# Loads of the tiles four ahead, tile 0's keys and values by ScalarE's queue, and the first expert's start inside the last retention tiles

## The chip, the cores and the metric

One core of a Trainium2 chip. The metric is the device time of one execution in microseconds (us); lower is better.

## The reference

Retention over 8 batches, 8 heads, 576 positions and a head width of 64, then a mixture of 16 experts (4 groups of 4), of which each token takes one. All in float32.

```python
scores = scale * np.matmul(q, k.transpose(0, 1, 3, 2))
ret = scores * Dmat[None, :, :, :]            # Dmat[h,i,j] = gamma_h ** (i-j) for i >= j, else 0
x = np.matmul(ret, v)                         # as 4608 tokens x 512
g_idx = argmax(x @ w_group); e_idx = argmax(x[g] @ w_expert[g])
h = np.maximum(x_e @ w1[g, e], 0.0)           # 512 -> 1024
out[tok_idx] = (g_w * e_w)[:, None] * (h @ w2[g, e])   # 1024 -> 512
```

## The kernel before

**Retention.** The tokens are 36 tiles of 128. Each tile has two inputs of 0.5 MB: `a` (queries and keys, transposed) and `b` (keys and values). In the loop's turn t TensorE (PE) makes `pst` (the running state, `state(t)`), `px` (the output of tile t-1, in two parts: `av(t-1)`, `inter(t-1)`), and `pss` (scores of tile t+1); ScalarE (ACT) scales the values (`vs`, eight small instructions) and copies the state (`st`); VectorE (DVE) masks the scores (`sT`) and takes `px` out of PSUM times a table `gq` (`xT`, `turned(t-1)`, line 704). `xT` is feature-major; PE transposes it back (`pxt`, `xnat_pe`, line 335), ACT weights it (`xt`), and GpSimd (POOL) scatters the 128 rows by an indirect DMA into a buffer in HBM, `xs`, one stretch of rows for each expert.

**Routing**, for three tiles at a time: `plt` (`logits`), `lt` (its copy on ACT), `pl` (`gate_pe`), a run of small DVE instructions that ends in `ob` (`choose`, line 385), `pp` (`places_pe`), the slots `sl` (`places`) and the weights `wt` (`weigh`). After tile 26's group (`PICK = 26`) `pick(0)` (line 478) counts the tokens with one small product `pc0` and chooses the expert that goes first; its number `e0i` is what SP reads before it can load that expert's weights. `pad0` is an indirect store that marks the first expert's spare rows.

**Experts.** Sixteen passes p, each with eight slices f: `ph` is layer 1 (`layer1(p, f)`, line 848), `hh` its ReLU, `py` layer 2 (`layer2`, line 888). Weights come as raw pieces `r1_p_i`, `r2_p_i` (512 KB each, two slices to a piece) and are split into a high and a low part (`wh` on ACT, `wl` on DVE), so that most products are made of three. The first pass is different: it takes the first 256 tokens of its expert, and its slices 0 to 5 use the raw weights unsplit. Tokens come back from `xs` as `xb` (`xload`, line 206), are transposed on DVE (`xturn`, line 252, to `xTf`) and split (`xsplit`: `xTh_m` on ACT, `xTl_m` on DVE). An `xb` load waits until the stores into its rows have landed. Results of a pass are transposed by DVE (`y`) and scattered to `out` by POOL. The last pass E = 16 (`last1`, `last_tr`, lines 954 and 970: `phn`, `hn`, `pth`, `hhn`, `py`) takes the rows that pass 0 left.

**What sets the order.** The order on each engine is the order of the calls: a wrapper (`Ordered`, line 106) ties every instruction to the one before it on its engine, so all have line 117 in the profile, and rows are told apart by tile names. SP issues the loads in the order of the calls. `a`, `b`, the weight pieces and `xb` share rings of buffers (tags `r1`, `r2`; `RB = 7`), and each load of a queue also waits for the completion of the load eight before it. Tile loads are asked for `LOADS - 1` = 6 tiles ahead: before the loop tiles 0 to 5, and then one in each turn.

**The places of the change.** Turns 31 to 36 of the loop carry `r = t - 26` = 5 to 10: the pick in t = 31, then `xload(0)` and one weight piece in each of t = 32 to 35, and `xturn(0)` in t = 35. After the loop pass 0 follows, with the routing and the stores of the last tiles between its slices. SP's `xload(1)` stands in slice 3 of pass 0.

Of the kernel before, what the change touches and what calls it, by code (L numbers as in the profile page):

```python
# [66 lines left out]
def moe_retention(ctx, tc, qk, kv, wgt, w1, w2, c_f, out):  # L67
# [779 lines left out]

    def layer1(p, f):
        i = p * NPIECE + f // 2
        C = CS[p]  # L850
        if (p, f) == (0, 0):
            ph = ps_st.tile([P, CMAX], F32, name=f"ph_{p}_{f}", tag="tr")
        elif p == 0:
            ph = psy.tile([P, CMAX], F32, name=f"ph_{p}_{f}", tag=f"py{f % 2}")
        else:
            pool_ = (ps_sm, ps_tr, ps_sm, ps_st)[f % 4]
            ph = pool_.tile([P, CMAX], F32, name=f"ph_{p}_{f}", tag="sm" if f % 2 == 0 else "tr")
        cs = slice((f % 2) * P, (f % 2) * P + P)
        hh = mp.tile([P, CMAX], F32R, name=f"hh_{p}_{f}", tag="hh", bufs=4)
        if whole(p, f):  # L860
            for kc in range(NKC):
                pe.matmul(
                    ph[:, :C], raws[i][0][:, kc, cs], xTf[p][:, kc, :C], start=kc == 0, stop=kc == NKC - 1
                )
            act.activation(hh[:, :C].bitcast(F32), ph[:, :C], AF.Relu)
            hts[p, f] = (hh.bitcast(F32), None)
            return
        wh, wl = wsp[i, 0]
# [498 lines left out]
```

## Time and profile before

| | |
|---|---|
| median of 3 runs | 609.99 us (607.59 to 610.55) |
| the profiled execution | 606.85 us |
| its span in the profile | 605.1 us |
| mean granted TensorE clock | 0.995 |
| PE busy | 584.0 us (97%) |
| DVE, ACT, POOL busy | 430.2 (71%), 325.2 (54%), 263.3 us (44%) |

Busy times are shares of the span of one execution. Starts are counted from the span's start, so the profiled execution's own time is 1.75 us more than its span.

### The profile page before, as it was taken

The page shows a single profiled execution, that of the slowest core. Times are in us where ns is not written, and L with a number is a line of the kernel's source. Part 1 is how long each engine was busy: PE and PEld are TensorE (multiplying, and loading weights), DVE is VectorE, ACT ScalarE, POOL GpSimd, SP SyncE. Part 2 cuts the span into 40 slices and gives each one's busy share as a digit, 9 for nine tenths or more (in the row PEclk, how much of TensorE's full clock was granted, in tenths as well). Part 3 has the DMA queues.
Part 4 walks back from the last instruction along what each step waited for, and adds up shares of the span by engine and source line. Part 5 has one row for each costly group of instructions (what it writes and reads, how often), then busy time and mean ns, then how long its engine had stood idle before and what let it go on. Part 6 is the DMA issues. An engine that isn't in the chain of part 4 may idle for free.

```text
span 605.1 us, 16614 instructions
## 1 busy us (share of the span) xinstructions
PE 584.0 (97%) x6191; PEld 549.7 (91%) x6191; DVE 430.2 (71%) x977; ACT 325.2 (54%) x849; POOL 263.3 (44%) x392
## 2 busy tenths in 40 slices
PE   7889999998999999999999999999999999999995
PEld 7778788777668999999999999999999999999994
DVE  3777677677477666997757675867768677686773
ACT  4677877865346434445435454544545455455553
POOL 0022322333313037494645537373563734636554
PEclk8999999999999999999999999999999999999999
DMA  8999999956983942819465563838467394674921
GB/s 332 416 384 341 344 344 337 353 183 194 381 261 97 349 199 77 298 40 340 111 265 146 230 235 145 284 115 311 130 245 249 123 334 118 259 240 153 369 93 35
DMA packets 62546, 143.11 MB, mean 237 GB/s; under 512 B 9313, under 2 KB 30185, under 8 KB 62464
## 3 DMA queue, kind: packets, MB, share of 16 engines
q1 hardware_dynamic: 53072, 121.59, 57.1%
q0 software_dynamic: 9248, 20.35, 9.4%
q8 instruction: 49, 0.80, 0.5%
q14 instruction: 33, 0.27, 0.1%
q10 hardware_dynamic: 144, 0.10, 0.1%
HBM read 121.67 MB, written 24.88 MB: 242 GB/s over the span
## 4 chain that ended last, share of the span: by engine, by line
PE 87%; DMA 5%; DVE 2%; issue 2%; POOL 1%; ACT 1%; SPq 0%; POOLq 0%; ACTq 0%; DVEq 0%
PE py L117 34%; PE ph L117 34%; PE px L117 7%; PE pss L117 4%; PE pxt L117 3%; PE pst L117 2%; DMA b<-in_kv 2%; PE plt L117 2%; POOL out L117 1%; DMA r<-in_w 1%; DMA xb<-xs 1%; DMA a<-in_qk 1%; PE pl L117 1%; DMA xs<-xt,sl 1%; PE phn L117 0%
## 5 line engine op out<-in xcount | busy, mean ns | idle before, releaser
L117 POOL DMA_INDIRECT out<-y,ii x152 | 167.2, 1100 | 51.0 <-issue 33.8
L117 DVE TENSOR_TENSOR wl<-r,wh 128x512 fp32r<-128x512 f32 x260 | 167.8, 687 | 8.3 <-ACT wh L117 4.5
L117 ACT ACTIVATE hh<-ph 128x356 fp32r<-128x356 f32 (+16 forms) x128 | 53.8, 420 | 212.6 <-PE ph L117 143.1
L117 PE MATMUL ph<-xTh_m,wh 128*128 128x356 f32 (+15 forms) x488 | 147.5, 302 | 0.8 <-ACT xTh_m L117 0.8
L117 ACT CAST wh<-r 128x512 fp32r<-128x512 f32 x260 | 146.9, 617 | 0.0
L117 PE MATMUL ph<-xTl_m,wh 128*128 128x356 f32 (+15 forms) x488 | 146.7, 301 | 0.1
L117 PE MATMUL ph<-xTh_m,wl 128*128 128x356 f32 (+15 forms) x488 | 146.6, 300 | 0.0
L117 PE MATMUL py<-hh,wh 128*128 128x288 f32 (+17 forms) x480 | 145.1, 302 | 0.0
L117 PE MATMUL py<-hl,wh 128*128 128x356 f32 (+14 forms) x480 | 144.7, 301 | 0.0
L117 PE MATMUL py<-hh,wl 128*128 128x356 f32 (+14 forms) x480 | 144.6, 301 | 0.0
L117 DVE SCALAR_TENSOR_TENSOR hl<-ph,hh 128x356 fp32r<-128x356 f32 (+15 forms) x122 | 56.7, 465 | 103.0 <-ACT hh L117 69.9
L117 POOL COPY pace<-hh 1x1 f32<-1x1 f32 x140 | 34.6, 247 | 140.4 <-ACT hh L117 138.4
L117 PEld LDWEIGHTS ph<-xTh_m,wh 128*128 128x128 f32 x488 | 92.0, 189 | 1.7 <-ACT xTh_m L117 1.2
L117 PEld LDWEIGHTS ph<-xTl_m,wh 128*128 128x128 f32 x488 | 92.0, 189 | 0.9 <-DVE xTl_m L117 0.4
L117 PEld LDWEIGHTS ph<-xTh_m,wl 128*128 128x128 f32 x488 | 92.2, 189 | 0.0
L117 PEld LDWEIGHTS py<-hh,wh 128*128 128x128 f32 x480 | 90.5, 189 | 0.2
L117 PEld LDWEIGHTS py<-hl,wh 128*128 128x128 f32 x480 | 90.4, 188 | 0.2 <-DVE hl L117 0.2
L117 PEld LDWEIGHTS py<-hh,wl 128*128 128x128 f32 x480 | 90.5, 189 | 0.0
L117 POOL DMA_INDIRECT xs<-xt,sl x36 | 35.9, 998 | 119.5 <-DVE ob L117 47.1
L117 ACT ACTIVATE vs<-b,cf 128x64 f32<-128x64 f32 x288 | 72.4, 335 | 7.9 <-DMA b<-in_kv 7.9
L117 DVE TENSOR_TENSOR sT<-pss,masks 128x512 f32<-128x512 f32 x72 | 46.0, 681 | 15.9 <-PE pss L117 10.7
L117 PE MATMUL px<-sT,vs 128*64 128x128 f32 x576 | 40.1, 280 | 2.2 <-DVE xT L117 1.7
(167 smaller groups left out, 615.8 us busy)
## 6 DMA issues: line engine op xcount, KB each, us to landing
r<-in_w SPq DMA_DIRECT2D x138, 512.0 KB
a<-in_qk SPq DMA_DIRECT2D x35, 512.0 KB
b<-in_kv SPq DMA_DIRECT2D x35, 512.0 KB
xb<-xs SPq DMA_DIRECT2D x24, 148.5 KB
xb<-xs SPq DMA_DIRECT2D x20, 165.0 KB
out<-y,ii POOLq DMA_INDIRECT x152
xb<-xs SPq DMA_DIRECT2D x12, 181.5 KB
xb<-xs SPq DMA_DIRECT2D x4, 198.0 KB
```

The costliest lines, as they stand in the source:

```text
L117: i_ = f(*a, **k)
```

## The change

- **Loads.** `LOADS` goes from 7 to 5. Tile 0's `b` is issued by ACT, values first, and not by SP; the table `gq` is loaded after tile 1's inputs and not before them; the gate's weights (`wgp`) and the rest of the constants (`cf`) are loaded after tile 3's inputs and not after tile 1's.
- **Turns 31 to 35.** Tile 26's `pxt`, `xt` and store move from t = 32 into t = 31, ahead of `pc0`, with a PSUM buffer of the pool of the small products (`ps_sm`, two buffers). Weight pieces 0 to 3 of the first expert are loaded one turn earlier, the first ahead of `xload(0)`. `xturn(0)` moves from t = 35 to t = 34, and the first product, `layer1(0, 0)`, from behind the loop to t = 35 between `inter(34)` and `turned(34)`.
- **Pass 0.** Its steps are reordered: `ph_0_1` comes first after the loop, `pl_35`, `choose` and `pxt_31` come behind the first `py`, and layer 2 of slice 5 comes ahead of layer 1 of slice 6. Two of the steps that rank the experts, `xpad(2)` and `xload(2)` move from pass 0 into pass 1.
- **Last pass.** `wh1_16_1` and `wl1_16_1` are split one step earlier.

```diff
-LOADS = 7
+LOADS = 5
@@ xnat_pe(t, pool_=None)
+        T["pxt"] = (pool_ or ps_tr).tile(
+            [P, NKC, P], F32, name=f"pxt_{t}", tag="sm" if pool_ else "tr"
+        )
@@ loads, t == 0
+                        if nm == "a":
+                            sp.dma_start(T[nm][:, i], src[nm][t, :, i])
+                        else:
+                            act.dma_start(T[nm][:, 1 - i], src[nm][t, :, 1 - i])
@@ before the loop
-            if t == 0:
+            if t == 1:
                 sp.dma_start(gqs[0], c_f[:, KC_GQ:KC_ALL].rearrange("p (x j) -> p x j", x=4))
-            if t == 1:
+            if t == 3:
                 sp.dma_start(wgp, wgt.rearrange("p (c e) -> p c e", c=NKC))
                 sp.dma_start(cf[:, KC_UP:KC], c_f[:, KC_UP:KC])
@@ the loop
                 inter(t - 1)
+                if r == 9:
+                    layer1(0, 0)
                 turned(t - 1)
...
+            if r == 5:
+                xnat_pe(PICK, ps_sm)
+                xnat_out(PICK)
...
-            if r in (6, 7, 8, 9):
+            if r in (5, 6, 7, 8):
                 if r == 6:
                     xload(0)
-                load_piece(r - 6)
-            if r == 9:
+                load_piece(r - 5)
+            if r == 8:
                 xturn(0, 0, 2)
                 xturn(0, 1, 2)
@@ passes
+            ahead = (p, f) == (0, WHOLE)
+            if ahead:
+                layer2(*prev)
             layer1(p, f)
...
+            if (p, f) == (0, 1):
+                gate_pe(NT - 1)
+                choose(NT - 1)
+                xnat(NT - 5)
             if (p, f) == (0, 2):
+                xnat(NT - 3)
                 tiles_counted()
-                xnat(NT - 2)
-                count_experts()
-            if (p, f) in ((0, 4), (0, 5)):
+            if (p, f) in ((0, 4), (1, 0), (1, 1)):
                 next(ranks, None)
...
+            if (p, f) == (1, 2):
+                xpad(2)
+            if (p, f) == (1, 3):
+                xload(2)
@@ last pass
         if pc == 0:
+            split(2 * E * NPIECE + 3)
             layer2(*prev)
```

On PE, turns 34 to 36 and the start of pass 0, before (`px_35` is in three rows by operand, `pp` left out):

```order
L117 MATMUL pxt_29_3107<-cf_64,xT_27_2494 128x128 x4
L117 MATMUL pl_32_3114<-cf_64,lt_32_3075 128x128 x3
L117 MATMUL px_35_3145<-sT_35_3060,vs_35_3006 64x128 x8
...
L117 MATMUL ph_0_0_3193<-xTf_0_3128,r1_0_0_2899 128x256 x4
...
L117 MATMUL plt_35_3212<-xT_33_3042,wgp_98 32x384 x4
L117 MATMUL pxt_30_3219<-cf_64,xT_30_2747 128x128 x4
L117 MATMUL pxt_31_3230<-cf_64,xT_30_2747 128x128 x4
L117 MATMUL pl_35_3241<-cf_64,lt_35_3217 128x128 x3
...
L117 MATMUL ph_0_1_3258<-xTf_0_3128,r1_0_0_2899 128x256 x4
```

and in the changed kernel:

```order
L117 MATMUL ph_0_0_3115<-xTf_0_3095,r1_0_0_2824 128x256 x4
L117 MATMUL pxt_29_3123<-cf_64,xT_27_2486 128x128 x4
L117 MATMUL pl_32_3130<-cf_64,lt_32_3079 128x128 x3
L117 MATMUL px_35_3152<-sT_35_3064,vs_35_3010 64x128 x8
...
L117 MATMUL ph_0_1_3200<-xTf_0_3095,r1_0_0_2824 128x256 x4
...
L117 MATMUL plt_35_3219<-xT_33_3046,wgp_98 32x384 x4
L117 MATMUL pxt_30_3226<-cf_64,xT_30_2747 128x128 x4
...
L117 MATMUL py_0_0_3260<-r2_0_0_2825,hh_0_0_3116 128x512
L117 MATMUL py_0_1_3261<-r2_0_0_2825,hh_0_0_3116 128x512
L117 MATMUL pl_35_3264<-cf_64,lt_35_3224 128x128 x3
L117 MATMUL pxt_31_3282<-cf_64,xT_30_2747 128x128 x4
```

The first product stands ahead of `px_35`, the second right behind it; `pl_35` is now behind the second product and the first `py`.

On PE in turn 31 (of the change: `pc0` is the small product of the pick, `px_31` is `av(31)`):

```order
L117 MATMUL plt_29_2775<-xT_27_2486,wgp_98 32x384 x4
L117 MATMUL pxt_26_2782<-cf_64,xT_24_2235 128x128 x4
L117 LDWEIGHTS ones_66
L117 MATMUL pc0_2802<-ob_9_2706,ones_66 128x16
L117 MATMUL px_31_2853<-sT_31_2684,vs_31_2620 64x128 x8
```

Before, `pc0` followed `plt_29` directly. `plt`, `pxt_26` and `pc0` now share the two buffers of `ps_sm`, so `pc0` takes the one that `plt_29` held.

On POOL, the last stores into `xs` ahead of pass 1 (of the change; before, `pad1` stood behind the store of `xt_34`):

```order
L117 DMA xs_63<-xt_33_3347,sl_35_3327 75776x528
L117 IOTA xt_34_3372 128x4x4
L117 DMA xs_63<-zero_82,pad1_79 75776x528
L117 IOTA xt_35_3395 64x4x4 x2
L117 DMA xs_63<-xt_34_3372,sl_35_3327 75776x528
L117 DMA xs_63<-xt_35_3395,sl_35_3327 75776x528
```

The store of `xt_35` is the last of the four in both.

## Rows read from the trace of the kernel before

**Rows 1.** The page's busy times: engine, busy us (share of the span), instructions.

```profile
PE 584.0 (97%) x6191; PEld 549.7 (91%) x6191; DVE 430.2 (71%) x977; ACT 325.2 (54%) x849; POOL 263.3 (44%) x392
```

**Rows 2.** Busy time by stretch: the stretch, its length, busy us of each engine (instructions), granted clock, DMA share, GB/s.

```profile
0.00:25.00 25.00, 20.78 (x430) 18.08 (x432) 13.49 (x27) 15.05 (x56) 1.02 (x8) 0.93 0.94 367
130.00:140.00 10.00, 9.15 (x190) 7.19 (x182) 8.33 (x30) 6.56 (x25) 4.65 (x8) 1.00 0.21 81
140.00:150.00 10.00, 8.63 (x179) 6.64 (x180) 7.32 (x22) 5.52 (x18) 3.55 (x6) 1.00 0.77 217
180.00:190.00 10.00, 8.91 (x47) 7.35 (x46) 9.27 (x26) 7.86 (x17) 2.10 (x2) 1.00 0.10 39
595.00:600.00 5.00, 3.31 (x14) 2.15 (x14) 1.07 (x4) 1.31 (x3) 3.06 (x4) 1.00 0.12 36
```

**Rows 3.** The start, ACT: start, us, what, and in brackets the idle time before it and its releaser. The `vs` are those of tiles 2, 4 and 6.

```profile
13.59 2.02 ACT L117 ACTIVATE vs<-b,cf 128x64 f32<-128x64 f32 x8 [1.05 <-DMA b<-in_kv]
...
19.16 2.02 ACT L117 ACTIVATE vs<-b,cf 128x64 f32<-128x64 f32 x8 [0.18 <-DMA b<-in_kv]
21.09 0.35 ACT L117 COPY st<-pst 128x256 f32<-128x256 f32 x1
...
25.20 1.07 ACT L117 ACTIVATE vs<-b,cf 128x64 f32<-128x64 f32 x4
```

**Rows 4.** The start, SP's issues (the first) and PE's states of tiles 2 and 4.

```profile
1.66 0.90 SPq L117 DMA_DIRECT2D b<-in_kv  x2
...
15.91 0.69 PE L117 MATMUL pst<-vs,b 128*64 128x64 f32 x16 [0.79 <-ACT st L117]
...
22.06 0.65 PE L117 MATMUL pst<-vs,b 128*64 128x64 f32 x16
```

**Rows 5.** Busy time by stretch as in group 2, in PE's first long wait and after it.

```profile
6.00:7.00 1.00, 0.00 (x0) 0.00 (x0) 0.98 (x2) 0.00 (x0) 0.00 (x0) 1.00 1.05 367
...
8.00:12.00 4.00, 4.00 (x58) 3.67 (x59) 0.70 (x2) 2.94 (x14) 0.00 (x0) 0.57 1.02 402
```

**Rows 6.** Turn 31: `pc0` and `px_31` on PE, the copy `lt_29` on ACT, the pick's first step, `xT_31` and `sT_33` on DVE.

```profile
131.58 0.18 PE L117 MATMUL pc<-ob,ones 128*128 128x16 bf16 x1
131.69 1.09 PE L117 MATMUL px<-sT,vs 128*64 128x128 f32 x16
...
132.34 0.47 ACT L117 COPY lt<-plt 128x384 f32<-128x384 f32 x1
...
134.65 0.68 DVE L117 TENSOR_TENSOR xT<-px,gq 128x512 f32<-128x512 f32 x1
136.23 1.29 DVE L117 TENSOR_TENSOR sT<-pss,masks 128x512 f32<-128x512 f32 x2 [0.90 <-PE pl L117]
```

**Rows 7.** Turns 34 to 36 and pass 0, PE's waits, and on DVE `xT_34`, `xturn(0)` and `xT_35`.

```profile
147.61 1.09 PE L117 MATMUL px<-sT,vs 128*64 128x128 f32 x16 [0.70 <-DVE xT L117]
150.00 1.97 PE L117 MATMUL ph<-xTf,r 128*128 128x256 f32 x8 [0.67 <-DMA r<-in_w]
154.29 0.66 PE L117 MATMUL pxt<-cf,xT 128*128 128x128 f32 x4 [0.83 <-ACT xt L117]
...
146.87 0.69 DVE L117 TENSOR_TENSOR xT<-px,gq 128x512 f32<-128x512 f32 x1 [2.37 <-PE pxt L117]
147.47 1.29 DVE L117 STREAM_TRANSPOSE xTf<-xb 128x512 f32<-128x512 f32 x2
```

**Rows 8.** Two pieces of SP's issues: the first expert's tokens and weights, and pass 2's tokens; and DVE's transposes of the latter.

```profile
141.39 1.92 SPq L117 DMA_DIRECT2D xb<-xs  x4
...
191.12 2.01 SPq L117 DMA_DIRECT2D xb<-xs  x4
...
206.13 1.76 DVE L117 STREAM_TRANSPOSE xTf<-xb 128x384 f32<-128x384 f32 x3
```

**Rows 9.** The chain that ended last, in order of time, from 165 to 182 us without PE's pieces: start, us, what.

```profile
168.89 3.90 DMA xs<-xt,sl
174.47 4.71 DMA xb<-xs
179.30 1.91 DVE xTf L117 x3
```

**Rows 10.** POOL's stores into `xs` at the end of pass 0 (`xt_33` and `xt_35`), SP's loads of pass 1's tokens, and PE's first product of pass 1.

```profile
164.35 0.99 POOL L117 DMA_INDIRECT xs<-xt,sl  x1 [3.27 <-ACT xt L117]
...
168.89 1.13 POOL L117 DMA_INDIRECT xs<-xt,sl  x1 [0.28 <-issue]
...
172.90 1.89 SPq L117 DMA_DIRECT2D xb<-xs  x4
...
181.77 0.43 PE L117 MATMUL ph<-xTh_m,wh 128*128 128x356 f32 x1 [0.76 <-ACT xTh_m L117]
```

**Rows 11.** The end: DVE's four transposes of pass 15, PE's wait for `wl1_16_1`, the first and the last of POOL's nine stores of pass 15, and its store of the last pass.

```profile
583.91 1.57 DVE L117 STREAM_TRANSPOSE y<-py 128x288 f32<-128x288 f32 x4
588.86 0.39 PE L117 MATMUL phn<-wl,xTh_m 128*128 128x256 f32 x1 [0.39 <-DVE wl L117]
...
585.76 0.97 POOL L117 DMA_INDIRECT out<-y,ii  x1 [6.34 <-DVE y L117]
...
597.31 0.97 POOL L117 DMA_INDIRECT out<-y,ii  x1 [0.30 <-issue]
599.61 0.97 POOL L117 DMA_INDIRECT out<-y,ii  x1 [1.33 <-ACTq L1182]
```

More of the change, by code (lines that the diff above doesn't have):

```diff
@@ L521, in without, with layer1 @@
         dve.tensor_scalar(mi0, sln, picked["c0"], float(BIG), ALU.is_ge, ALU.mult)
+    def layer1(p, f):
+        i = p * NPIECE + f // 2
+        C = CS[p]
+        if (p, f) == (0, 0):
+            ph = ps_st.tile([P, CMAX], F32, name=f"ph_{p}_{f}", tag="tr")
+        elif p == 0:
+            ph = psy.tile([P, CMAX], F32, name=f"ph_{p}_{f}", tag=f"py{f % 2}")
+        else:
+            pool_ = (ps_sm, ps_tr, ps_sm, ps_st)[f % 4]
+            ph = pool_.tile([P, CMAX], F32, name=f"ph_{p}_{f}", tag="sm" if f % 2 == 0 else "tr")
+        cs = slice((f % 2) * P, (f % 2) * P + P)
+        if (p, f) == (0, 0):
+            hh = wp.tile([P, NKC, EARLY], F32, name="hh_0_0", tag="wl0", bufs=3)[:, 0]
+        else:
+            hh = mp.tile([P, CMAX], F32R, name=f"hh_{p}_{f}", tag="hh", bufs=4)
+        if whole(p, f):
+            for kc in range(NKC):
+                pe.matmul(
+                    ph[:, :C], raws[i][0][:, kc, cs], xTf[p][:, kc, :C], start=kc == 0, stop=kc == NKC - 1
+                )
+            hf = hh if f == 0 else hh.bitcast(F32)
+            act.activation(hf[:, :C], ph[:, :C], AF.Relu)
+            hts[p, f] = (hf, None)
+            return
+        wh, wl = wsp[i, 0]
+        xh, xl = xTs[p]
+        n = 0
+        for kc in range(NKC):
+            for a, b in ((wh, xh), (wh, xl), (wl, xh)):
+                pe.matmul(
+                    ph[:, :C], a[:, kc, cs], b[:, kc, :C], start=n == 0, stop=n == 3 * NKC - 1
+                )
+                n += 1
+        C32 = 32 * nblocks(p)
+        if f == 0 and C32 > C and not natural(p):
+            dve.memset(hh[:, C:C32].bitcast(F32), 0.0)
+        hl = mp.tile([P, CMAX], F32R, name=f"hl_{p}_{f}", tag="hl", bufs=4)
+        act.activation(hh[:, :C], ph[:, :C], AF.Relu)
+        dve.scalar_tensor_tensor(
+            hl[:, :C], ph[:, :C], 0.0, hh[:, :C].bitcast(F32), ALU.max, ALU.subtract
+        )
+        hts[p, f] = (hh, hl)
     obs = []
@@ L757, in moe_retention @@
             late_consts(t)
-            if now and 6 <= t:
+            if now and 6 <= t and r != 6:
                 xnat_pe(t - 6)
@@ L771, in moe_retention @@
                 u -= 1
-            for u in range(max(u + 1, 0), t - 5):
+            for u in range(max(u + 1, 0), t - 5 + (r == 5)):
                 if now:
@@ L845, in rank_experts @@
         dve.tensor_scalar(mil, el, cr[:, 0:1], float(BIG), ALU.is_ge, ALU.mult)
[L848 to L868, printed above, removed]
-        xh, xl = xTs[p]
-        n = 0
-        for kc in range(NKC):
-            for a, b in ((wh, xh), (wh, xl), (wl, xh)):
-                pe.matmul(
-                    ph[:, :C], a[:, kc, cs], b[:, kc, :C], start=n == 0, stop=n == 3 * NKC - 1
-                )
-                n += 1
-        C32 = 32 * nblocks(p)
-        if f == 0 and C32 > C and not natural(p):
-            dve.memset(hh[:, C:C32].bitcast(F32), 0.0)
-        hl = mp.tile([P, CMAX], F32R, name=f"hl_{p}_{f}", tag="hl", bufs=4)
-        act.activation(hh[:, :C], ph[:, :C], AF.Relu)
-        dve.scalar_tensor_tensor(
-            hl[:, :C], ph[:, :C], 0.0, hh[:, :C].bitcast(F32), ALU.max, ALU.subtract
-        )
-        hts[p, f] = (hh, hl)
     def layer2(p, f):
```

47 lines of the change are left out of this document (23 added, 24 removed).

## The prediction

> **What bounds the kernel now.** I read the busy times first: PE is busy for 584.0 of the span's 605.1 us [rows 1], so all its idle time together is 21.1 us, and no reordering that leaves PE's work as it is can win more. The change adds no product and takes none away. Then the busy time by stretch, to see where that idle time lies [rows 2]: 25.00 - 20.78 = 4.2 us in the first 25 us, 0.85 + 1.37 = 2.2 us between 130 and 150 us, with a wait of 0.83 behind it [rows 7] 3.05 us, then 1.09 us from 180 to 190, and 1.69 us from 595 to 600. The change touches all four places. Then, for each place, which wait ends last there.
>
> At the start it is a transfer: ACT scales the values of tiles 2 and 4 as soon as they land, at 13.59 and 19.16, and not before tile 6 does it find them there without waiting [rows 3]; PE's state of tile 2 waits for ACT's copy behind the scaling [rows 4]. The DMA engines are busy for 0.94 of the stretch at 367 GB/s [rows 2]. In the transition PE has three waits of 0.70, 0.67 and 0.83 us [rows 7]. Behind them another chain ends last, without PE: POOL's store of tile 35 at 168.89, its landing 3.90 later, the tokens of pass 1 (issued from 172.90, the last piece 4.71 us under way), and their transposes at 179.30 for 1.91 us [rows 9, 10]. PE's first product of pass 1 stands at 181.77, after a wait of 0.76 [rows 10]. At the end it is POOL: nine stores paced from 585.76 to 597.31 and the last pass's at 599.61 [rows 11].
>
> **The change part by part.** Times are of the profiled execution, 606.85 us.
>
> *Loads asked for four ahead.* On SP the tiles' loads keep their order, and each still waits for its buffer and for the load eight before it. So the smaller number by itself moves no transfer: 0. What moves at the start is the order of bytes. `wgp` (128 x 128) and the rest of `cf` (128 x 517 floats) are 64 + 265 = 0.33 MB that now go behind tile 3's inputs; at 367 GB/s [rows 2] tiles 2 and 3 land 0.9 us earlier. Tile 4's inputs have the same bytes ahead of them as before, so its scaling still starts near 19.16; with 2.02 for it and 0.35 for the copy [rows 3] PE's state of tile 4 can follow at 21.5 where it stood at 22.06 [rows 4]. That is **-0.5**, though tile 2 alone would give -0.9. What waits for `wgp` is the routing of tiles 0 to 2, which comes behind tile 4's state: hidden.
>
> *The second queue.* SP's two issues of tile 0's `b` took 0.90 us from 1.66 [rows 4]. ACT issues them after its exponential's table, about 1 us later, values first. The engines that move the bytes are busy from there on (1.05 of the stretch from 6 to 7 us [rows 5]), so an earlier issue of tile 1 by 0.90 buys nothing: 0. A tile 0 that is 1 us late is covered, because the end of the stage is set by tile 4. The bounds of the whole start: -1.0 if nothing of tile 4 binds, +0.4 if tile 0's lateness is passed on to tile 2's scaling.
>
> *Turn 31.* `pc0` now takes the PSUM buffer that `plt_29` held, and so waits for ACT's copy `lt_29`, which ends at 132.34 + 0.47 = 132.81; before, it ran at 131.58 [rows 6]. That is 1.2 us, with `px_31` queued behind it on PE. DVE's pick follows, and `xT_31` behind it at 134.65; masking of tile 33 stood at 136.23 after 0.90 of idle time, which swallows part [rows 6]. PE's old wait there goes as well. I take +0.55, with the bounds 0 and +1.35.
>
> *Turns 34 to 36.* `ph_0_0` (1.97 us) now fills the 0.70 in which `px_35` waited for `xT_34`, and the 0.67 for the weights goes, since they are asked for two turns earlier [rows 7]: -1.37. What is late next: `ph_0_1`, now right behind `px_35`, takes the PSUM bank that `px_35` was in, and so waits for `xT_35` on DVE, which is queued behind the routing of tile 32. From the row of `xT` (0.68 us) and its handover I put that at about 1.1 us of PE's idle time. So up to there the sum is +0.55 - 1.37 + 1.1 = +0.3. Behind it the 0.83 [rows 7] goes, because the transposes of tiles 30 and 31 no longer stand together: PE comes to slice 4 some 0.5 us earlier.
>
> *What pass 1 waits for.* This is another chain. `pl_35` now stands behind the second product and the first `py`, some 2.3 us later, but `pp_35`, which needs its result, stood at PE's turn and comes about 0.4 us earlier. POOL's store of tile 33 stays near 164.35 [rows 10]; behind it stand `pad1`, tile 34 and tile 35, each 0.99 and 0.3 of issue, so tile 35's store goes at 164.35 + 3 x 1.3 = 168.3 instead of 168.89: -0.6. Its landing, the tokens and their transposes cost what they cost [rows 9]. So pass 1 starts **-0.6** earlier, and PE, which gets there earlier still, waits longer than 0.76. Bounds: -2.5, if that chain shortens with all of PE's 3.05 us of idle time less 0.55; +1.4, if the wait of turn 31 passes whole. A wait of 1.1 to 1.3 us there is the sign that PE's gain had no taker.
>
> *Pass 2's tokens.* They were issued at 191.12 and turned at 206.13 without a wait [rows 8]; issued some 3 us later, with 6.4 us (172.90 to 179.30, [rows 9, 10]) to land, they are there by 201: 0.
>
> *The end.* The split ahead takes away PE's 0.39 [rows 11] and a like gap ahead of it, at most 0.75. But on DVE it stands ahead of the four transposes, 1.57 us in all, and POOL's first store waits for them [rows 11]; a split of 1.29 us comes in front, and the paced stores end that much later: 597.31 + 0.97 + 1.29 = 599.57, with 0.3 to the last store, 599.87 against 599.61. I take **+0.2**; bounds -0.75 (the pace tightens) and +0.3.
>
> **The sum** is -0.5 - 0.6 + 0.2 = -0.9, so 605.95 for the profiled execution. That execution stands 3.1 below the median of the runs, 609.99, and the four executions shown have a mean of 608.75; I put the forecast at that level: 608.75 - 0.9 = 607.85, say **607.9 us**.
>
> **The rivals.**
> *A: the gains pass whole.* If tile 35's store follows PE (its PSUM and weights ready earlier) and the end tightens: -1.0 - 2.5 - 0.75 = -4.25, so 604.5. For it: every wait named is on PE, and PE is 97% busy. Against it: POOL's fixed pace between 164.35 and 168.89, and at the end.
> *B: tile 0's tokens of pass 0 come too late.* `xturn(0)` now stands ahead of `xT_34` on DVE. Before, `xT_34` began at 146.87 after 2.37 idle [rows 7]; with 1.29 for the transposes they must have landed by 145.58. They were issued at 141.39 [rows 8]; if they go no earlier, behind the weights that are now ahead of them, and take 6.4, they land at 147.8: 2.2 us late, and `px_35` waits with them. After a wait of that kind at the start (PE idle the whole of 6 to 7 us) the granted clock fell to its lower level, 1.2 GHz for part of it, with a mean of 0.57 from 8 to 12 us [rows 5], which costs 4 x 0.43 = 1.7 us. Then -0.5 + 0.55 + 2.2 + 1.7 - 0.8 + 0.2 = +3.35, slower: 612.1. Against it: the store that the load waits for now goes ahead in turn 31, so the load should go near 139.5, and decides only if it is later than about 139.2 with a 6.4 us flight; in a quiet queue (81 GB/s from 130 to 140 [rows 2]) the flight should be shorter.
> The Trainium skill ("TensorE: Matmul & The Clock Gate", the section on HAM oscillation) says that a wait of PE for DMA lets its clock drop and that the work behind it starts at the lower rate. By that rule the three short waits of the transition would cost clock already; the trace differs, with 1.00 granted from 140 to 150 us [rows 2]. In the sum the clock is therefore charged at nothing.
> *C: nothing.* The loads are gated by buffers, not by issue; if tile 1's transfer shares the engines with tile 0's and the turn-31 wait passes whole, -0.5 + 0.8 - 0.6 + 0.2 = -0.1: 608.7.
>
> **How the numbers follow.** Forecast 0.50, A 0.22, C 0.17, B 0.11. The range takes in A's and most of B, 604.6 to 611.8; beyond it lie the ends of both. 0.5%, about what a measurement of this kernel can tell from no change, is 3.05 us. Most of A is faster by more; of the forecast about a quarter (the runs scatter by 3 us, and the level was taken below their median); most of B slower: faster 0.32, same 0.57, slower 0.11.
>
> **What would show it.** Right: PE's state of tile 4 near 21.5; a wait of `pc0` of about 1.2 us for `lt_29`; none of `px_35`; a wait of `ph_0_1` for `xT_35` near 1 us; tile 35's store near 168.3 and pass 1 near 181.2; POOL's first store of pass 15 near 587. Wrong: `xturn(0)` waiting for its tokens, a clock below 1.00 near 148 us, pass 1 before 180, or a store of pass 15 that starts no later.

## The result, and the profile after

| | before | changed kernel |
|---|---|---|
| median, 16 runs each on one chip | 610.01 us (606.13 to 613.65) | 614.18 us (611.45 to 617.88) |
| ratio | 1 | 1.0086 [1.0068, 1.0105] |
| the profiled execution, its span | 606.85, 605.1 us | 613.49, 611.7 us |
| its mean granted clock | 0.995 | 0.989 |

The change is slower by 4 to 6 us. Forecast were 607.9 and a range that ended at 611.8. The page's busy times of the changed kernel (engine, busy us, share, instructions) answer to [rows 1]:

```profile
PE 585.2 (96%) x6191; PEld 551.5 (90%) x6191; DVE 430.8 (70%) x977; ACT 325.1 (53%) x849; POOL 262.2 (43%) x392
```

PE's work is the same (1.2 us more busy time, same count), so 5.4 of the 6.6 us by which the span is longer are idle time of PE. Busy time by stretch (columns as in [rows 2]), with four microseconds behind PE's longest wait added, tells where:

```profile
0.00:25.00 25.00, 20.02 (x424) 18.05 (x424) 13.49 (x26) 14.88 (x55) 1.02 (x8) 0.86 0.95 371
130.00:140.00 10.00, 8.23 (x178) 6.44 (x176) 6.71 (x25) 6.42 (x22) 4.66 (x8) 1.00 0.29 92
140.00:150.00 10.00, 8.97 (x196) 6.88 (x192) 8.76 (x26) 6.21 (x22) 2.29 (x4) 1.00 0.77 228
180.00:190.00 10.00, 6.80 (x39) 5.96 (x38) 7.30 (x15) 4.00 (x10) 0.00 (x0) 0.91 1.07 340
188.00:192.00 4.00, 4.00 (x15) 3.67 (x14) 4.00 (x10) 3.81 (x10) 0.00 (x0) 0.57 0.76 311
```

From 180 to 190 us PE is idle for 3.20 us, where it was idle for 1.09 [rows 2], and the clock that was granted behind that, from 188 to 192 us, is 0.57. PE's timeline (start, us, what, and in brackets the wait before it and its releaser) names the places; the rows are tile 4's state, `pc0`, `ph_0_0`, `px_35`, `ph_0_1` and the first product of pass 1:

```profile
22.40 0.73 PE L117 MATMUL pst<-vs,b 128*64 128x64 f32 x16
...
134.51 0.17 PE L117 MATMUL pc<-ob,ones 128*128 128x16 bf16 x1 [0.68 <-ACT lt L117]
...
149.72 1.97 PE L117 MATMUL ph<-xTf,r 128*128 128x256 f32 x8 [0.38 <-issue]
152.38 1.09 PE L117 MATMUL px<-sT,vs 128*64 128x128 f32 x16
...
155.97 1.99 PE L117 MATMUL ph<-xTf,r 128*128 128x256 f32 x8 [1.87 <-DVE xT L117]
...
186.93 0.43 PE L117 MATMUL ph<-xTh_m,wh 128*128 128x356 f32 x1 [3.07 <-ACT xTh_m L117]
```

`px_35` no longer waits, `pc0` and `ph_0_1` do, and the wait before pass 1 has grown from 0.76 [rows 10] to 3.07 us. POOL's timeline shows what that wait is for (rows: the stores of tiles 31 and 33, the index fill of `xt_34`, the store of `pad1`, the store of tile 35; then the first and the last store of pass 15):

```profile
164.21 0.99 POOL L117 DMA_INDIRECT xs<-xt,sl  x1 [2.02 <-ACT hh L117]
...
168.21 0.99 POOL L117 DMA_INDIRECT xs<-xt,sl  x1 [1.16 <-ACT xt L117]
...
171.25 0.15 POOL L117 IOTA xt<- 128x16 int32 x1 [2.05 <-DMA xs<-xt,sl]
172.04 0.99 POOL L117 DMA_INDIRECT xs<-zero,pad  x1 [0.64 <-issue]
...
174.94 1.37 POOL L117 DMA_INDIRECT xs<-xt,sl  x1 [0.30 <-ACT hh L117]
...
593.35 1.42 POOL L117 DMA_INDIRECT out<-y,ii  x1 [7.98 <-DVE y L117]
...
606.22 0.97 POOL L117 DMA_INDIRECT out<-y,ii  x1 [0.30 <-issue]
```

Tile 35's store goes 6.73 us behind tile 33's; before, it went 4.54 behind [rows 10]. In between, the index fill of `xt_34` waits 2.05 us for a landing. Three buffers serve all `xt`, so tile 34's is the one of tile 31, whose store must have landed. The chain that ended last has that landing and, later, the tokens of pass 1 (start, us, what):

```profile
164.21 6.98 DMA xs<-xt,sl
...
179.77 4.56 DMA xb<-xs
...
184.46 1.91 DVE xTf L117 x3
```

The flight of the tokens and the transposes are as they were [rows 9]: all of the delay lies ahead of SP's load.

### The profile page after: what moved, and what is told of

It reads as the page before. It is cut to its first block, busy times and chain, and to the rows that moved or that the text cites. A ratio compares the mean times of both kernels' runs of the same rounds, so it can differ in the third digit from the quotient of the medians.

```text
span 611.7 us, 16608 instructions
## 1 busy us (share of the span) xinstructions
PE 585.2 (96%) x6191; PEld 551.5 (90%) x6191; DVE 430.8 (70%) x977; ACT 325.1 (53%) x849; POOL 262.2 (43%) x392
## 4 chain that ended last, share of the span: by engine, by line
PE 89%; DVE 3%; DMA 3%; issue 2%; POOL 1%; ACT 1%; another core or an unknown queue 0%; SPq 0%; ACTq 0%; POOLq 0%; DVEq 0%
PE py L117 34%; PE ph L117 34%; PE px L117 9%; PE pss L117 4%; PE pxt L117 3%; PE pst L117 2%; PE plt L117 2%; DMA xs<-xt,sl 1%; DMA b<-in_kv 1%; POOL out L117 1%; DMA xb<-xs 1%; PE phn L117 1%; DVE xT L117 1%; PE pl L117 1%; DVE sT L117 0%
## 5 line engine op out<-in xcount | busy, mean ns | idle before, releaser
L117 POOL COPY pace<-hh 1x1 f32<-1x1 f32 x140 | 32.5, 232 | 139.4 <-ACT hh L117 137.0
L117 PEld LDWEIGHTS px<-sT,vs 128*64 128x64 f32 x576 | 31.6, 139 | 13.2 <-issue 8.7
```

The lines of the kernel that those rows point to most:

```text
L117: i_ = f(*a, **k)
```

## The experiments

The kernels of one group ran on one chip beside their own runs of the kernel before, whose medians were 607.46, 606.95, 606.13, 607.25 and 607.33 us in groups 1 to 5. Ratios are to that kernel, with 95% intervals; they are as recorded with the runs and not the quotients of the medians, from which they differ by up to 0.002 (e10: 607.23 over 606.13 is 1.0018). Diffs are against the changed kernel unless said otherwise. The first execution of every kernel was profiled, and from each trace three legs are taken that begin and end on the same instructions in all kernels: from `xT_30` to `xT_33` (turn 31), from there to PE's first product of pass 1 (the transition), and from there to the first product of the last pass (the passes).

| kernel | turn 31 | transition | passes | ratio |
|---|---|---|---|---|
| before (predicted from) | 12.94 | 39.15 | 402.60 | |
| before again (e19) | 11.97 | 41.24 | 402.87 | |
| before's middle: e3, e4, e7 | 11.98, 11.97, 11.97 | 42.01, 43.40, 43.47 | 402.73, 402.75, 402.93 | 0.9988, 1.0001, 0.9993 |
| change, three profiles (first, e5, e13) | 14.69, 12.56, 12.56 | 40.97, 42.01, 42.58 | 403.76, 404.59, 403.18 | 1.0086, 1.0037, 1.0026 |
| e1, e9, e10 | 12.56, 12.57, 12.58 | 41.77, 41.56, 41.10 | 404.95, 404.47, 403.71 | 1.0013, 1.0022, 1.0039 |
| e11, e17 | 12.57, 12.56 | 41.03, 41.06 | 403.72, 402.78 | 1.0024, 1.0007 |
| e2, e12 | 11.99, 12.57 | 47.35, 45.02 | 403.68, 402.77 | 1.0119, 1.0084 |
| e8, e16, e14 | 12.56, 12.55, 12.54 | 41.51, 39.75, 39.79 | 402.78, 402.76, 402.73 | 0.9982, 0.9998, 0.9984 |
| e15, e18 | 12.55, 12.57 | 38.13, 38.27 | 402.60, 402.85 | 0.995, 0.994 |

In the two profiles of the last section the 6.6 us between the spans are 1.6 ahead of `xT_30`, 1.75 in turn 31, 1.8 in the transition, 1.2 in the passes and 0.3 behind them. The 1.6 tell nothing: `xT_30` comes between 126.6 and 131.3 us in the sixteen profiles with the change's start.

**Group 1: each part by itself.** The start and the end alone, in the kernel before:

```diff
-LOADS = 7
+LOADS = 5
...
-                        sp.dma_start(T[nm][:, i], src[nm][t, :, i])
+                        if nm == "a":
+                            sp.dma_start(T[nm][:, i], src[nm][t, :, i])
+                        else:
+                            act.dma_start(T[nm][:, 1 - i], src[nm][t, :, 1 - i])
... (and the places of gq, wgp and cf)
```

> The kernel before, with only the start changed (loads asked four ahead, tile 0's keys and values by ACT's queue, gq and the constants later). In the changed kernel xT of tiles 1 and 2 came 0.4 and 0.5 us earlier, and that of tiles 4 to 24 0.3 to 0.55 later, with a mean granted clock of 0.79 from 10 to 20 us against 0.92. Theory C (the clock stays low longer and eats the gain): xT of tiles 5 to 24 0.3 to 0.6 us late, ratio 1.0005 to 1.001. Theory of the prediction: tile 4's state near 21.5 and tiles 5 to 24 earlier by 0.5 us, ratio 0.999.

```diff
+            split(2 * E * NPIECE + 3)
             layer2(*prev)
...
-            split(2 * (E * NPIECE + pc) + 3 + k)
+            split(2 * (E * NPIECE + pc) + 4 + k)
```

> The kernel before, with only the last pass's early split. The prediction: +0.2 us, since POOL's first store of pass 15 starts 1.3 us later and the paced stores end that much later; ratio 1.000 to 1.001. Rival: PE's gap of 0.75 goes and the stores keep up: -0.7 us, ratio 0.9985 to 0.9995.

e3: 606.57 us, 0.9988 [0.9963, 1.0013]. e4: 607.80, 1.0001 [0.9975, 1.0026]. Neither can be told from no change, and neither costs the 1.0086. Tile 26's store back in t = 32:

```diff
-            if now and 6 <= t and r != 6:
+            if now and 6 <= t:
                 xnat_pe(t - 6)
...
-            if r == 5:
-                xnat_pe(PICK, ps_sm)
-                xnat_out(PICK)
```

> The changed kernel, with only turn 31 put back: tile 26's pxt in turn 32, so that pc0 does not wait for lt_29. In the changed kernel xT_32 is 1.75 us later against before than xT_30 (3.34 - 1.59). Theory L: those 1.75 us pass through to the last stores and to pass 1, and the time falls by 1.5 to 2.5 us: ratio 1.005 to 1.006. Theory R: the stores of tiles 30 and 31 still stand behind the first two products, the iota of tile 34 still waits for a landing, and the time falls by under 1 us: ratio 1.007 to 1.009.

e2: 615.21, 1.0119 [1.0089, 1.0148]. Turn 31 is at its old length (11.99), but the transition takes 47.35 us. Its trace is rival B in the main, late tokens and then the lower clock. The rows are SP's load of the tokens, POOL's store of tile 27, DVE's transposes and `ph_0_0`:

```profile
142.45 1.41 SPq L117 DMA_DIRECT2D xb<-xs  x3
...
143.13 0.99 POOL L117 DMA_INDIRECT xs<-xt,sl  x1 [4.74 <-DVE mi L117]
...
149.30 1.30 DVE L117 STREAM_TRANSPOSE xTf<-xb 128x512 f32<-128x512 f32 x2 [4.89 <-DMA xb<-xs]
...
150.70 2.90 PE L117 MATMUL ph<-xTf,r 128*128 128x256 f32 x6 [4.80 <-issue]
```

So the move of tile 26's steps is what keeps rival B away. With it SP's load waits for `pad0`'s landing and no longer for tile 26's store, and goes 11.2 us behind `xT_30` (e5) instead of 11.9 (e2); tile 27's store goes 13.2 behind it instead of 12.6. So the two stand 2.0 us apart and not 0.7. The third part, the ring of `xt`, was taken out of the way with a buffer that is free there:

```diff
-        xt = T["xt"] = gp.tile([P, Q, WQ], F32, name=f"xt_{t}", tag="xt", bufs=3)
+        if t < NT - 2:
+            xt = gp.tile([P, Q, WQ], F32, name=f"xt_{t}", tag="xt", bufs=3)
+        else:   # tiles 34 and 35: halves of one buffer of the pool of y
+            ... xlast["b"] = mp.tile([P, NB, DQ], F32, name="xt_last", tag="y", bufs=2)
```

> The changed kernel, with only the buffers of xt_34 and xt_35 taken outside the ring of three. In the changed kernel POOL's iota of tile 34 waits for the landing of tile 31's store (164.21 + 6.98 = 171.2), with pad1 and the last two stores queued behind it, and tile 35's store goes at 174.94 instead of 168.89. Theory R (the ring of three xt buffers makes pass 1 late): tile 35's store moves from 174.94 to 171 to 172, PE's wait for xTh_m before pass 1 falls from 3.07 to under 1 us, its clock stays at 1.00, and the time falls by 3 to 4 us: ratio to before 1.002 to 1.004. Theory L (PE's waits of turn 31 and for xT_35 make everything late, the ring follows): POOL's stores move by under 1 us and the time by under 1 us: ratio 1.007 to 1.009.

e1: 608.05, 1.0013 [0.999, 1.0036]. Of POOL's timeline the stores of tiles 33 and 35, of SP's the load of pass 1's tokens, of PE's the first product:

```profile
161.62 0.99 POOL L117 DMA_INDIRECT xs<-xt,sl  x1 [1.17 <-ACT xt L117]
...
165.97 0.97 POOL L117 DMA_INDIRECT xs<-xt_last,sl  x1 [0.30 <-issue]
...
171.83 1.91 SPq L117 DMA_DIRECT2D xb<-xs  x4
...
180.96 0.67 PE L117 MATMUL ph<-xTh_m,wh 128*128 128x356 f32 x1 [3.70 <-ACT xTh_m L117]
```

The index fill no longer waits and the store goes 4.35 us behind tile 33's, about as before the change. But SP's load follows it by 5.86 us where it was 4.01 before [rows 10] and 3.25 in the changed kernel, and PE waits 3.70. The ring made the store late, as I read it, but it is not the only bound: without it the landing takes longer and pass 1 comes no earlier.

**Group 2: the change again, and its order of pass 0.** The unchanged changed kernel, and the buffer of e1 in the kernel before:

```diff
(e5: none. e7: the edit of e1, in the kernel before)
```

> The changed kernel once more, on the chip of the next three, since one profiled execution differs from another by some us in the retention loop alone (the kernel with only two more xt buffers had xT_30 at 126.63, the changed one at 131.27, on the same code up to there). All theories: ratio 1.007 to 1.010. Theory R: tile 34's iota on POOL again waits 1 to 3 us for the landing of a store of tile 31, and tile 35's store again goes 6 us or more behind tile 33's. Theory L: that wait is absent or under 0.5 us, and the lateness is in place before tile 33.

> The kernel before, with only the buffers of xt_34 and xt_35 taken outside the ring of three. Theory R: in the order before, tile 31's store goes 8 us ahead of tile 34's, so the ring holds nothing up, and the ratio is 0.998 to 1.001; the gain of two more buffers belongs to the changed order. Rival (two more buffers are worth 4 us in any order): 0.993 to 0.995.

e5: 608.98, 1.0037 [1.001, 1.0063]; e7: 607.47, 0.9993 [0.9966, 1.0019]. e5's trace has the wait (the fill of `xt_34` on POOL, PE's first product of pass 1) and the clock behind it again:

```profile
166.34 0.15 POOL L117 IOTA xt<- 128x16 int32 x1 [3.06 <-DMA xs<-xt,sl]
...
181.89 0.66 PE L117 MATMUL ph<-xTh_m,wh 128*128 128x356 f32 x1 [3.30 <-ACT xTh_m L117]
```

```profile
182.00:186.00 4.00, 4.00 (x13) 3.73 (x14) 4.00 (x9) 3.36 (x8) 0.00 (x0) 0.50 0.99 405
180.00:200.00 20.00, 18.11 (x91) 17.38 (x92) 15.36 (x37) 11.08 (x23) 4.17 (x4) 0.83 0.53 182
```

In its turn 31 `pc0` finds `lt_29` ready; it runs behind `pxt_26`, which the change put ahead of it (PE's two rows, and ACT's of `lt_29`):

```profile
129.22 0.66 PE L117 MATMUL pxt<-cf,xT 128*128 128x128 f32 x4
129.89 0.17 PE L117 MATMUL pc<-ob,ones 128*128 128x16 bf16 x1
...
129.36 0.48 ACT L117 COPY lt<-plt 128x384 f32<-128x384 f32 x1
```

Then pass 0 in the old order, with the moves of the loop kept (`layer1(0, 0)` is skipped in the passes, since the loop has done it); and, in the new order, the transposes of tiles 30 and 31 ahead of the second product:

```diff
-            if (p, f) == (0, 0):
-                prev = (p, f)
-                continue
-            ahead = (p, f) == (0, WHOLE)
...
+            if (p, f) != (0, 0):
+                layer1(p, f)
... (every other step of the passes' loop as in the kernel before)
```

> The changed kernel, with the passes' order put back to that of before; the start, turn 31, the earlier weights and tokens, the first product in turn 35 and the end stay changed. Theory R (pass 0's order puts tile 31's transpose behind two products and makes the ring bind): tile 35's store goes 4.5 us behind tile 33's, pass 1 starts 3 to 5 us earlier than in the changed kernel, ratio 0.998 to 1.003. Theory L (pc0's wait and the early tokens on DVE): ratio 1.006 to 1.010.

```diff
+            if (p, f) == (0, 1):
+                xnat_pe(NT - 6)
+                xnat_pe(NT - 5, ps_sm)
+                xnat_out(NT - 6)
+                xnat_out(NT - 5)
             layer1(p, f)
... (their stores ahead of pick(1))
```

> The changed kernel, with only the transposes and stores of tiles 30 and 31 moved ahead of ph_0_1, into PE's wait for xT_35; the ring stays at three buffers. Theory R: tile 31's store goes near 160 instead of 164.2, its landing is past when tile 34's iota comes, tile 35's store moves 2 to 3 us forward, ratio 1.000 to 1.004. Theory L: nothing before pass 0 is touched, so the lateness stays: 1.006 to 1.009.

e8: 605.60, 0.9982 [0.9958, 1.0007]; e9: 608.67, 1.0022 [0.9994, 1.005]. The old order takes the loss away, by 0.0055 against e5 beside it. Moving two transposes does not take PE's wait before pass 1 away, which is 4.00 us in e9 (the fill of `xt_35` now waits 2.27 us for a landing); its ratio can be told neither from e5's nor from 1.

**Group 3: the clock, the weights, a combination.** One weight piece asked for behind the tokens of pass 1 rather than ahead; 26 products that nobody uses ahead of pass 1; e8 with the piece late and with `lt_29` ahead of `xt_25` on ACT, to shorten `pc0`'s wait:

```diff
(e10, e12, e14)
-                new = {2: (4, 5), 3: (6,), 5: (7,)}.get(f, ())
+                new = {2: (4, 5), 4: (6,), 5: (7,)}.get(f, ())
(e11; e17 with range(56))
+            if (p, f) == (1, 0):
+                pw2 = ps_tr.tile([P, P], F32, name="pw2", tag="tr")
+                for i in range(26):
+                    pe.matmul(pw2, ones, ones, start=True, stop=True)
             layer1(p, f)
(e12, beside the order of e8)
                 xnat_pe(t - 6)
+                if r == 5:
+                    logits(t - 2)
                 xnat_out(t - 6)
```

> The changed kernel, with only the third weight piece of pass 1 loaded behind that pass's tokens instead of ahead of them. So far every kernel with the changed pass order has PE waiting 3.1 to 4.0 us for the tokens of pass 1, also with two more xt buffers, where tile 35's store went 4 us earlier but took 5.9 us to land instead of 3.0. Theory D (the landing is what waits, since 3 MB of weights are under way when the stores go out): with 1 MB less ahead, the wait at pass 1 falls by 1.5 to 3 us, and the ratio falls by 0.003 to 0.006 against the changed kernel of this same call. Theory R (the ring and POOL's pace): the wait stays above 3 us and the ratio within 0.002.

> The changed kernel, with 26 small products (128 x 128, their result unused) put on PE ahead of pass 1's first product, where PE otherwise waits over 3 us. They add about 2.9 us of PE time inside that wait and no byte. Theory C (the wait itself is not the whole cost: the clock falls behind it, 0.83 over 180 to 200 us in three of five profiles): the granted clock stays at 1.00 from 180 to 200 us, and the time falls by 1.2 to 2.2 us, ratio lower by 0.002 to 0.0035 than the changed kernel's of this call. Rival (the clock's loss is small or the products lie in the way): within 0.001, or slower by up to 1 us.

> The kernel with the passes' order of before and the rest of the change (ratio 0.998 in the last call), with two more edits: the copy lt_29 ahead of xt_25 on ACT in turn 31, so that pc0 waits 0.6 us less, and the third weight piece of pass 1 behind that pass's tokens. Expected of the sum of the theories: turn 31's +0.58 us (xT_30 to xT_33: 12.56 against 11.97) goes, PE waits under 1 us before pass 1, clock 1.00: ratio 0.995 to 0.998. If theory D is wrong and the pick's wait costs nothing: 0.997 to 1.000.

> The changed kernel a third time, beside the three others of this call: 1.0086 in the first measurement and 1.0037 in the second. Ratio 1.002 to 1.009; PE's wait before pass 1 at 3 to 4 us, its clock from 180 to 200 us at 0.83 to 0.92, and xT_30 to xT_33 at 12.5 to 14.7 us.

e10: 607.23, 1.0039 [1.0012, 1.0065]: no gain that can be told from the change beside it (e13), and PE still waits 2.94 us. e11: 608.48, 1.0024 [0.9998, 1.005]: the 26 products took 1.62 us, left a wait of 1.68, and 0.50 was granted from 184 to 186 all the same; by itself inconclusive. e13, the change once more: 608.85, 1.0026 [1.0, 1.0052]. e12 was a miss, 611.13, 1.0084 [1.0062, 1.0107], and told more than the others. Turn 31 did not get shorter (12.57). SP's load, POOL's store of tile 27 and DVE's transposes:

```profile
143.41 0.87 SPq L117 DMA_DIRECT2D xb<-xs  x2
...
143.78 0.99 POOL L117 DMA_INDIRECT xs<-xt,sl  x1 [5.11 <-DVE mi L117]
...
150.13 1.30 DVE L117 STREAM_TRANSPOSE xTf<-xb 128x512 f32<-128x512 f32 x2 [5.07 <-DMA xb<-xs]
```

The tokens take 6.72 us from the load to the transposes, with a store of POOL's 0.37 behind the load. This is rival B again, by what follows in group 4 from a swap of two small ACT instructions.

**Group 4: what to keep.** e12 without the swap on ACT; e8 again; the clock with 56 products; and e8 with the product put back behind the loop:

```diff
(e15, e18, beside the order of e8)
                 inter(t - 1)
-                if r == 9:
-                    layer1(0, 0)
                 turned(t - 1)
...
-            if r == 8:
+            if r == 9:
                 xturn(0, 0, 2)
```

> The kernel with the passes' order of before and the rest of the change (0.998), with only the third weight piece of pass 1 behind that pass's tokens. The last call's kernel had this and the copy lt_29 ahead of xt_25, and came out at 1.008: its tokens for pass 0 were asked 1.5 us later against tile 33, 0.4 us ahead of tile 27's store, and took 6.7 us instead of 4.7. Theory S (tokens that go out within 0.7 us of a store of tile 27 take 7 us, those 1.8 us or more ahead of it 4.7 to 4.9): without the moved copy the tokens go 1.8 us ahead again, DVE waits 1.0 to 1.6 us for them, ratio 0.996 to 1.000. Rival (the moved weight piece did it): 1.006 to 1.009.

> The kernel with the passes' order of before and the rest of the change, once more beside the others: 0.998 in its first measurement. If the pass order is what makes the changed kernel slower, 0.996 to 1.000 again, with PE's wait at pass 1 under 1 us and the clock at 1.00 from 180 to 200 us. If that was scatter between calls, up to 1.004.

> The changed kernel with 56 small unused products ahead of pass 1's first product, where 26 took 1.62 us and left a wait of 1.68, behind which the clock still fell to 0.50 for about 3 us. 56 take 3.5 us. Theory C: the wait left is under 0.6 us, the granted clock stays at 1.00 from 180 to 200 us, from pass 1's first product to the last pass's it takes 402.7 us instead of 403.2 to 404.6, and the ratio falls to 0.999 to 1.002 (the changed kernel: 1.0086, 1.0037, 1.0026). Rival (the clock is no part of it): 1.003 to 1.009.

> The kernel with the passes' order of before and the rest of the change, with the first product and its tokens' transposes put back behind the loop and into turn 35: so only the store of tile 26, the weights and the tokens are early. Theory S: the tokens have landed when DVE comes to them in turn 35, PE's wait for the first product (3.0 us in three of four profiles of the order before) falls under 0.7, the order xT_34, transposes on DVE costs px_35 its old wait of 0.7: ratio 0.994 to 0.998. Rival (the early product is what gains): no better than 0.998 to 1.001.

e14: 605.75, 0.9984 [0.9953, 1.0015], so the swap was what cost e12 its 5 us. e16: 607.41, 0.9998 [0.9965, 1.0031]; its transition is 1.76 us shorter than e8's, the same kernel, in whose profile three microseconds from 155 to 158 us were granted 0.50. e17: 607.41, 1.0007 [0.9976, 1.0038]; its PE rows (the unused products, pass 1's first) and the stretch behind them:

```profile
177.72 3.30 PE L117 MATMUL pw<-ones 128*128 128x128 bf16 x56
...
181.26 0.43 PE L117 MATMUL ph<-xTh_m,wh 128*128 128x356 f32 x1 [0.24 <-ACT xTh_m L117]
```

```profile
180.00:200.00 20.00, 19.42 (x126) 18.22 (x123) 14.83 (x36) 11.31 (x25) 4.66 (x4) 1.00 0.60 191
```

Pass 1 starts about as late as in the change (a transition of 41.06 us), the clock stays at 1.00, and the passes take 402.78 us as in the kernel before, where the change's three profiles have 403.18 to 404.59. All twenty profiles agree: in the twelve with a clock of 1.00 over the first ten microseconds of pass 1 the passes take 402.60 to 402.93 us, in the eight with 0.50 in part of them 403.18 to 404.95. So I put 0.4 to 1.8 us of the loss down to the clock, behind a wait that PE spent idle. The steps that the change moved into pass 1 are in e17 too, so they are not what makes the passes longer.

e15: 604.64, 0.995 [0.9922, 0.9977]. Its rows are SP's load, POOL's store of tile 27, `xT_34` and the transposes, `ph_0_0`, and pass 1:

```profile
140.78 1.39 SPq L117 DMA_DIRECT2D xb<-xs  x3
...
142.85 0.99 POOL L117 DMA_INDIRECT xs<-xt,sl  x1 [6.15 <-DVE mi L117]
...
145.70 0.69 DVE L117 TENSOR_TENSOR xT<-px,gq 128x512 f32<-128x512 f32 x1 [1.57 <-issue]
146.31 1.29 DVE L117 STREAM_TRANSPOSE xTf<-xb 128x512 f32<-128x512 f32 x2
...
148.12 1.99 PE L117 MATMUL ph<-xTf,r 128*128 128x256 f32 x8
...
180.39 0.43 PE L117 MATMUL ph<-xTh_m,wh 128*128 128x356 f32 x1 [1.15 <-ACT xTh_m L117]
```

Nothing waits for the tokens, pass 1 waits 1.15 us, and the clock is 1.00 in every ten microseconds from 130 to 200.

**Group 5: repeats.** The same kernel as e15, and the kernel before with a profile:

```diff
(e18: as e15. e19: none, the kernel before)
```

> The fastest kernel so far once more (tile 26's store, weights and tokens early; first product and passes as before; start and end of the change): 0.995 in its first measurement. If that holds: 0.992 to 0.998, with no wait of PE for the first product.

> The kernel before, unchanged, for a second profile of it. The prediction was made from one in which DVE found the tokens of pass 0 landed; the three kernels that have the same order there and differ elsewhere waited 2.9 to 3.5 us for them. Theory S: this one waits too, 2.5 to 3.5 us, PE's first product behind it, with tile 27's store within 0.7 us of the tokens' load. If the first profile is the typical one: no wait, as there.

e18: 603.88, 0.994 [0.9923, 0.9957], so the gain repeats on another chip. e19, one run, 605.98. Its load, store, transposes and `ph_0_0`, and PE's clock behind:

```profile
138.90 1.93 SPq L117 DMA_DIRECT2D xb<-xs  x4
...
139.93 0.99 POOL L117 DMA_INDIRECT xs<-xt,sl  x1 [4.72 <-DVE mi L117]
...
146.03 1.30 DVE L117 STREAM_TRANSPOSE xTf<-xb 128x512 f32<-128x512 f32 x2 [2.56 <-DMA xb<-xs]
...
147.39 3.22 PE L117 MATMUL ph<-xTf,r 128*128 128x256 f32 x8 [2.12 <-DVE xTf L117]
```

```profile
148.00:151.00 3.00, 3.00 (x16) 2.11 (x18) 2.69 (x14) 0.55 (x2) 0.00 (x0) 0.50 0.97 353
```

The profile that the prediction was made from had no such wait [rows 7]; in e19 and the other three profiles with before's order there (e3, e4, e7) DVE waits 2.56 to 3.46 us for these tokens and PE 2.12 to 3.40 at `ph_0_0`; what comes last for PE is the transposes in e19 and e4, and in e3 and e7 a weight piece, 0.5 and 1.0 us behind the transposes. The first one was the exception: its store of tile 27 went 1.83 us behind the load (143.22 against 141.39 [rows 8]), theirs 0.50 to 1.03 us.

## Why the prediction was wrong, point by point

- **Turn 31: the size right, the reason not.** Forecast +0.55, measured 12.56 against 11.97, +0.59. It was to be a wait of `pc0` for `lt_29` of 1.2 us, partly swallowed. Except in the first profile of the change `pc0` shows no wait: it stands 1.45 us behind the start of `plt_29` instead of 0.78, of which 0.66 is `pxt_26`, now ahead of it on PE; `lt_29` ends 0.05 us before. That the size fits is luck. In the first profile the leg is 14.69; 2.1 us of that came in no other (0.68 is `pc0`'s wait for `lt_29`, 1.38 a wait of DVE's mask of tile 33 for a releaser that the trace doesn't name) and have no cause that I can show.
- **Waits of the transition: the parts nearly as forecast, the balance not.** `px_35` waits for nothing, `ph_0_1` waits for `xT_35` (forecast 1.1; 1.87 in the first profile, about 1.1 in the others). But the gain was counted against 0.70 + 0.67 + 0.83 [rows 7], the waits of an execution that is not the usual one. Usually the kernel before loses 2.1 to 3.4 us at `ph_0_0`, and the change takes most of that away (0.38, 1.33 and 1.33 us are left in its three profiles). That was a larger gain than I had in the sum.
- **Pass 1 at -0.6: wrong, and the first step that failed.** It rested on tile 35's store at 168.3, three paced stores behind tile 33's. I charged POOL's issue of the four steps only, not the buffer that the first of them, the fill of `xt_34`, waits for: it waited 2.05, 3.06 and 3.18 us in the three profiles. The forecast wait before pass 1 was 1.1 to 1.3 us; it is 3.07, 3.30 and 3.92. e1 shows that the ring is one bound of two, since with it gone the landing of the store filled the time (why it takes 5.86 us there is open; weights that are under way then are a guess, and e10, which moved one piece, shows no gain). What removes the wait is the old order of pass 0: 0.55, 0.57 and 0.55 us in e8, e16 and e14, with transitions of 41.51, 39.75 and 39.79. Which of the reordered steps does it was not separated. The prediction's sign, pass 1 near 181.2, is -0.6 in all, while its sum adds the start's -0.5 to that.
- **The clock at nothing: wrong.** I had three waits under 0.9 us with a clock of 1.00 behind them [rows 2, 7] and let them stand for the wait before pass 1, which by my own sum was to be longer. Behind the waits of 3 to 4 us the lower level was granted, with 0.50 or 0.57 in the rows above, and against e17 that is 0.4 to 1.8 us. With the wait as forecast, 1.1 to 1.3 us, a charge of nothing would have been right: the clock stayed at 1.00 behind 1.15 (e15), 1.30 (e18) and 1.54 us (e7). So this term failed because the wait was mis-sized. The Trainium skill ("TensorE: Matmul & The Clock Gate", the section on HAM oscillation) tells of a kernel whose long waits of PE for DMA were each followed by work at the lower rate. The trace agrees for the long waits, if not always from their end: in the first profile 0.83 was granted in the first 2 us of pass 1 and 0.50 in the next two. The page does not say it of every short wait, so the three short ones of the transition, which the prediction held against it, were no test of it.
- **The two together.** Between `xT_33` and pass 1 three profiles of the change have a mean of 41.85 us and five with before's order 41.85: what was won at `ph_0_0` is lost at pass 1. (That they agree so closely is chance: the five lie between 39.15 and 43.47.) From `xT_30` to pass 1, where the forecast was -0.6, the means are 55.1 against 54.0, +1.1, and the passes add another 1.1: from `xT_30` to the last pass 458.97 against 456.80 in the same profiles, +2.2 us. That is the size of e5 and e13 (1.0037 and 1.0026 of 607, so 2.2 and 1.6 us).
- **Rival B: not in the change, but near.** It was given 612.1 us, 3.35 above its level (with a -0.8 in its sum for which it names no row); where it happened in full it cost 7.2 us (e2, the whole kernel) and 5.1 us (e12), some 5 to 6 us above the kernels without it (e5 and e13; e8 and e14). In the change DVE waits 0.47, 1.42 and 1.43 us for the tokens. The reason that I gave against it, the early store of tile 26, is what e2 shows, but not by its size: the load was to go 1.9 us earlier, at 139.5. Against `xT_30` it goes at 11.2 us (e5, e13) where before's order has 11.5 to 12.1, and of the 1.3 us by which the distance to tile 27's store is wider than in e2, 0.6 come from turn 31, which delays that store.
- **Start: earlier at tile 4, not shown in the time.** The tile 4 state came at 22.40, not 21.5, with a clock of 0.86 from 0 to 25 us where it had been 0.93 [rows 2]. But the sixteen profiles with this start have it at 21.3 to 22.4, and the four without at 22.1 to 24.6. At `xT_30` nothing of that can be seen: means of 129.0 and 128.2 us. ACT's issue of tile 0's `b` came at 1.24 us, beside its table load (1.18 to 2.46), and not about 1 us after SP's 1.66. e3's interval, -2.2 to +0.8 us, holds both the forecast of -0.5 and nothing, with the second queue in it.
- **End: as forecast within what can be told.** POOL's first store stands 2.66 us behind the last pass's first product (590.69), where it stood 1.39 behind; 1.27 later, against 1.29 forecast. The rest absorbs it: from that product to the span's end it is 21.0 us against 20.7, and e4 gives 1.0001.
- **Pass 2's tokens at nothing:** the traces agree, since e17 loads them late too and its passes take 402.78 us; it was not tried by itself.

**Still open** is why the first measurement gave 1.0086 and two repeats 1.0037 and 1.0026, 3 us less. The clock of its 16 runs has a median of 0.989 (e5 0.9915, e13 0.994), and 0.005 x 612 is about 3 us, so the difference may be clock; what lowers it there no run shows. The 2.1 us of turn 31 in its one profile are the other candidate. By the repeats the forecast of 0.9 us less was off by 2.5 to 3.1 us only, and that is luck: a loss at pass 1 and a gain at `ph_0_0`, neither of that size in the sum, nearly cancel.

The best of the kernels run is e15 (e18): tile 26's store, the weights and the tokens early, the product and the order of pass 0 as before. It beats the kernel before by 0.5 and 0.6%.

## What to carry to other kernels

When a step moves on a queue, look at what its buffer waits for as well as at the pace of the queue: here a ring of three made a reordered fill wait 2 to 3 us. Then look for the next bound: without the ring (e1) pass 1 came no earlier. A product that is put into a gap earlier does not shorten a chain that another engine's stores end; it only moves PE's wait, and a wait made of many short ones may come back as one long one that also costs clock. Take several profiles of the kernel before, since one execution can show a place without the wait that it usually has.

## What the runs showed of the hardware

- **A load and a store close together.** From SP's load of the first tokens to DVE's transposes it is 4.7 to 5.0 us in the ten profiles in which DVE waited for it and POOL's next indirect store went 1.89 to 2.37 us behind the load, and 4.9 in the first of the change (3.14 behind). In the six in which it went 0.37 to 1.03 us behind, it is 6.7 to 7.6 us. e12 against e14 shows both from one swap; that the store itself is what slows the load was not tried.
- **PE's clock behind waits.** Ahead of pass 1 it stayed at 1.00 behind waits of PE of 0.24 to 1.54 us (twelve profiles), and behind `ph_0_1`'s 1.87 in the change too; behind 2.12 (e19, at `ph_0_0`) and behind each wait of 2.94 to 4.00 us ahead of pass 1 (seven profiles) rows of a few microseconds show 0.50. One wait's length does not tell alone: two stretches of 1.6 us, busy and then idle (e11), ended at 0.50, and behind three waits of 0.36, 0.43 and 0.91 us in pass 0 0.50 was granted in e8, while the same kernel kept 1.00 behind the same three in e16 (0.36, 0.42, 0.90).
- **Landings.** From an indirect store of one tile to what waited for it took 2.8 us (e10, tile 35, to SP's load) to 8.2 us (e13, tile 31, to the fill of `xt_34`), and 3.25 and 7.04 us for the same two places in one profile, the first of the change.
